# Gated linear attention and a gated MLP on one core: every chunk handled in pairs, attention's output summed already turned in 64x32 tiles

## The chip, the cores and the metric

The kernel runs on one core of a Trainium2 chip. The metric is the device time of one execution in microseconds (us); the kernel before takes 144.32 us, the median of three runs (144.17 to 144.49). TensorE multiplies matrices and writes to PSUM (eight banks of 128 partitions x 512 fp32 here), VectorE, ScalarE and GpSimd work on SBUF (GpSimd not on PSUM), and SyncE issues nearly all DMAs. In the profile these are PE (PEld for its weight loads), DVE, ACT, POOL and SP.

## The reference

```python
# attention: B=4, H=8, S=768, D=48, alpha in (0.8, 1)
for t in range(S):
    state = alpha[:, :, t, :, None] * state + einsum('bhd,bhe->bhde', k[:, :, t], v[:, :, t])
    y[:, :, t] = einsum('bhd,bhde->bhe', q[:, :, t], state)
x = y.transpose(0, 2, 1, 3).reshape(B, S, 384)
# gated MLP: d_ff = 1024, w_spatial is 768x768
h = maximum(x @ w_in, 0);  u, v = h[..., :512], h[..., 512:]
v_n = (v - mean(v)) / sqrt(var(v) + 1e-6)
v_s = einsum('ts,bsd->btd', w_spatial, v_n) + b_spatial[None, :, None]
out = (u * v_s) @ w_out
```

Inputs and output are fp32; matmuls work on bf16.

## The kernel before

**Attention in chunks.** A batch's 768 steps are six chunks of 128, 24 chunks in all. In a chunk the recurrence is turned into matmuls: the logarithm of alpha (`ln`) is summed over time by a matmul with a triangle of ones (`cum`), ScalarE takes exp(-sum) (`einv`) and exp(sum) (`eexp`, in place in PSUM), k is multiplied by the first (`kt`) and q by the second (`qt`). TensorE transposes both (`tr`, `trk`), DVE or ACT copy them to SBUF (`ev`, tile kqT). The scores (`sc`) are k against q for each head, masked on DVE (`m`, tile ptm). The output y of a chunk is scores times v plus q times the state at the chunk's start (`ya`, `y`). The state (`upd` on TensorE, `z` on DVE, decay `S` and block-diagonal bf16 copy `sb` on POOL) goes from chunk to chunk. The heads are taken two by two, `HP` = 4 pairs of heads, each head in 64 columns or rows of which 48 are used.

**Two forms.** The first eight chunks run in `pair(j)` (line 423, `PAIRS` in line 53): one load brings 256 steps, step 2p and 2p+1 side by side in partition p, so that 384 bytes lie together in memory. Chunk 0 of the pair is then partitions 0 to 63 and chunk 1 partitions 64 to 127, each with an even and an odd half (`par`). The sums over time take two matmuls for each half, with `le_pair` and `lt_pair` (line 461); `upd` (553), `sc` (583), `ya` (610) and `y` (623) take a chunk from half of the rows. The other 16 chunks run in `first(i)` (line 634), one chunk at a time: loads of 192 bytes a row, `cum` in line 666, totals in 669, transposes of k and q in 64-row halves (719), `upd` in 740, `sc` in 754, `y` in 776 (state part) and 782 (scores times v).

**To the MLP.** y stands in PSUM with time in the partitions. The MLP needs x with features in the partitions, so `finish_x` (line 356) has ACT copy y to x_sb, TensorE transpose it (374 in pairs, 398 elsewhere), and ACT or DVE copy it out into xT:

```python
363 def xs(eng):
364     st["x_sb"] = work.tile([128, KS, 128], BF16, name="x_sb")
365     copy(eng, st["x_sb"], st["y"]...)            # 128x384, fp32 to bf16
...
373     for ks in range(KS):
374         nc.tensor.transpose(xv[:, ks, :], st["x_sb"][:, ks, :], ident)
```

**The MLP.** All its matmuls have line 828: v (three of 512 columns for 128 steps), u (three of 384), the mixing s with w_spatial turned (six of 384; two steps `part 0` and `part 1` after the normalised v of tiles 0 to 3 and 4, 5), and the output o (four of 384). `second_v` has DVE take batch-norm statistics (893, 894), except for four tiles named in `ACT_STATS` (line 54), where ACT sums (879, 889) and DVE finishes (905 to 908). `se` adds the bias (976), `g` multiplies with u (989). Lines 197, 199 and 205 are the helpers for copies on ACT, on DVE or POOL, and relu on DVE. w_in, w_out and w_spatial are loaded in fp32 pieces and cast; w_spatial is turned by TensorE (`wt`, 840).

**The order.** Each step is an `Op` with its engine; the string `PLAN` lists all steps in the order in which they are issued, with the letter of the engine (P, D, A, G for GpSimd, S for SyncE). An engine does its own steps in this order and waits where an input isn't ready. A word such as `P53:512:512:192` puts fill matmuls ahead of a step: products of a constant fp32 tile (`junk`, line 187) of so many columns, whose result isn't used. PSUM banks are taken in turn.

Of the kernel before, what the change touches and what calls it, by code (L numbers as in the profile page):

```python
# [14 lines left out]

class Op:


    def __init__(self, key, eng, dur, emit, deps=(), prio=0.0, take=None, lat=0.13, cols=0):  # L20
        self.key = key
        self.eng = {eng: dur} if isinstance(eng, str) else dict(eng)
        self.emit, self.prio, self.lat, self.cols = emit, prio, lat, cols
        self.take = [take] if isinstance(take, Slot) else list(take or ())
        self.deps = [d for d in deps if d is not None]
        self.done = False
        self.big = False


class Ring:  # L30


    def __init__(self, bufs):
        self.bufs = bufs


class Slot:
    def __init__(self, ring):
        self.ring, self.users = ring, []


ENGINES = {
    "kt": {"POOL": 0.9},
    "vb": {"POOL": 0.48, "ACT": 0.42},
    "S": {"POOL": 0.5},
    "sb": {"POOL": 0.73, "DVE": 0.95},
    "vn": {"DVE": 0.42},
    "xe": {"ACT": 0.4},
    "ev": {"DVE": 0.34, "ACT": 0.48},
    "u": {"ACT": 0.39, "DVE": 0.49},  # L50
    "o": {"ACT": 0.4},
}
PAIRS = (0, 1, 2, 3)
ACT_STATS = ((2, 2), (1, 4))
LETTERS = {"P": "PE", "D": "DVE", "A": "ACT", "G": "POOL", "S": "SP", "Q": "DMA"}

PLAN = """
S34 Q35 S36 Q37 G32 G0 Q33 S38 Q39 S94 Q95 S40 Q41 A42 P53:512:512:192 A54 D1 D2 D56 P43 S96 Q97 S98 Q99 S100 Q101
S163 Q164 S4 Q5 S165 Q166 S167 Q168 P59:464 G58 G48 A44 A45 A55 D46 D57 D47 P249:304 P49 P61 A50 P51 D52 D60 A62 A102
A250 P71:304 P74 P113 P103 D72 D73 D76 D75 P63 P77:172 D65 A114 D116 P119:148 A104 A64 A115 A105 A78 G66 G67 G106 D107  # L60
D117 D68 P79 P81 P111 P121 P247 P109 G3 G69 A108 A82 A80 D120 D122 D112 D110 P83 A84 A171 D248 S169 Q170 S9 Q10 S307
Q308 P131 P134 D133 D136 D132 D135 G70 G118 P172:228 P182 P123:240 A183 A8 A173 A124 P137 P138 A139 A174 G7 G6 D125
P85 G126 D128 D185 G127 G129 G175 P88 P142 P140 A86 A184 D176 D186 A143 A89 P188 P190 P180 P144 P178 A141 A191 A145
A181 P146 G11 G12 S309 Q310 S311 Q312 D130 D87 D179 D90 D189 P157 A187 A177 A158 A147 A13 P197 P200 P192 D199 D201
D198 D194 D202 P151:196 P155 A315 A193 A91 P326 P316 A327 P203 P153 P204 G195 G196 G329 A317 A328 A318 P149 A205 A154
D159 D156 D152 D330 G319 P208 P334 A209 P206 D320 P332 P324 P210 P322 D92 D335 D325 D333 D148 A207 P212 A211 A150 P347
P215 P221 A213 A160 A222 A216 S14 Q15 P223 P227 S18 Q19 D93 D323 D161 D348 D349 D214 G16 G17 A224 A228 P225 P229 A226
A21 P232 A234 D231 D230 D233 G20 P235:300 P238 S313 Q314 G331 G321 P344 P336 S367 Q368 S369 Q370 S22 Q23 S371 Q372
A237 A236 D217 D162 D346 A240 D338 A239 A218 D219 D220 A375 A337 P251 P263 P259 P376 A377 A378 G339 P264 D345 D341
D265 P260 D261 P255 P252 A380 A25 A24 D381 D253 P256 D257 G340 G342 G379 S409 Q410 S373 Q374 S446 Q447 S411 Q412 S413  # L70
Q414 S415 Q416 S26 Q27 S480 Q481 S448 Q449 S482 Q483 S450 Q451 S484 Q485 P383 A385 A417 S452 Q453 S577 Q578 S486 Q487
S581 Q582 S579 Q580 S583 Q584 P244 P241 P350 A246 D384 D245 D242 D243 P390 P354 P418 D392 D391 A351 A355 G262 G343
A420 A382 G254 G266 P279 P352 P271 P356 P393 P272 A353 A357 A419 G421 A422 A394 P280 P361 P386 P275 P395 A362 A424
A396 A31 D273 D423 D281 D387 P425 D397 D427 D426 D363 G282 G388 P276 P358 D277 P398 G258 G389 G278 G30 A399 A454 A359
A28 A488 P405 P432 P267 P455 P401 A402 A457 A456 D29 P291 P489 P268 A490 A459 D406 D433 D400 D434 D360 P283 P428 D269
D460 A492 D429 D493 G458 G491 P435 A284 A292 A436 G274 G461 G270 G430 G431 S648 Q649 S617 Q618 S650 Q651 S611 Q612
S652 Q653 S613 Q614 S690 Q691 S615 Q616 S694 Q695 S654 Q655 S692 Q693 P287 P462 P437 P495 P403 D463 D464 D497 D496
A288 A439 A438 P440 A585 A441 A364 D404 P469 P498 P295 P465 P586 P303 D471 D470 D466 D500 D499 A296 A587 A588 A590
A304 P299 G494 G467 G468 G589 G592 D591 D442 P472 A473 P501 P407 P474 A502 A300 P503 P593 P596 A443 A505 A408 D475
D476 P477 A478 D504 D366 D594 D595 D445 D444 D597 D365 P506 P600 P515 D601 D516 A507 A479 A508 D509 D602 A656 A510  # L80
A619 P517 P525 P513 P519 P529 P657 P533 P620 D511 D512 P526 P530 A514 A659 A658 A621 A661 A622 A698 A624 D518 D520
D527 D531 D662 P545 P534 P699 A701 A700 A703 D625 G598 G599 G660 G626 G623 G528 D535 P546 D547 P630 P627 P664 P537
P603 D631 D665 D704 G548 A629 A628 G632 G663 A604 P538 P634 P605 S728 Q729 S762 Q763 S696 Q697 S730 Q731 S732 Q733
S764 Q765 S766 Q767 D539 A607 A666 A606 D635 D636 P541 P667 P542 G702 G532 P706 P671 D668 D543 D673 D672 G669 G536
G670 G544 G633 P608 P637 P521 A707 A736 A708 A638 P737 P713 P639 P522 P549 D714 D715 D641 D523 A770 A609 A705 A738
A739 G740 A640 A741 D742 P771 P550 P642 A772 P709 P744 A774 A643 A746 D710 D551 D775 D745 D644 G524 S858 Q859 S734
Q735 S929 Q930 S860 Q861 G773 G711 G552 G712 G743 G540 P716 P674 A717 A675 P561 P718 P676 P777 P553 A562 A678 A677
D719 D779 D720 D610 P679 P751 A778 A554 A866 A680 A645 A681 P780 D752 P747 D748 D753 D781 D782 P682 P867 P721 P754
A868 A869 A871 A722 A755 S768 Q769 S862 Q863 A723 A776 D683 D872 P573 P688 P684 G749 G750 G870 P756 P874 D646 D757
D875 D685 D758 A689 A574 D724 A876 P686 P783 P569 P881 A784 P785 A570 A787 A687 A725 D882 D786 D883 P759 P557 A760  # L90
P788 P565 P796 P798 P800 S1042 Q1043 S971 Q972 S892 Q893 S864 Q865 S898 Q899 S896 Q897 A979 A558 A789 A566 A937 A900
S894 Q895 S935 Q936 G873 S975 Q976 S931 Q932 S933 Q934 S973 Q974 S977 Q978 S1008 Q1009 S567 Q568 S1046 Q1047 S559 Q560
S1012 Q1013 S1010 Q1011 S1044 Q1045 S1014 Q1015 D727 D647 D761 D726 P794 P806 D790 A791 D799 D797 D795 D792 D793 D801
P901 P980 P802 P938 P877 P807 A902 A903 A907 A905 A981 A939 A940 A982 A944 A984 P810 P803 A942 G904 D878 G941 G879
D808 D906 D804 G805 G880 G809 G983 D985 D943 P822 P884 P811 D812 A885 P823 P908 P886 P945 D824 P814 P911 P815 D912
D909 D816 G813 G817 G913 G825 A910 A887 A888 A947 A946 P889 A1016 A890 P952 P915 P987 D953 D916 D954 P830 P1017 P831
P818 A988 A1019 A1050 A1018 D917 P948 P819 P1051 D949 A1021 A986 A989 D1022 D832 G950 P834 A1052 G951 G1020 P990 P842
P918 A835 A1054 D820 D991 D1055 A843 A919 P838 P1024 P994 P920 D1025 D921 D995 D996 A839 A1023 G914 G833 G1053 G992
S1048 Q1049 S575 Q576 S836 Q837 S844 Q845 S293 Q294 S289 Q290 S571 Q572 S305 Q306 S301 Q302 S555 Q556 A922 A1026 S297
Q298 S285 Q286 S840 Q841 P826 P955 P827 D828 A956 P1057 P957 P1031 D958 P1027 D1028 D1033 D1032 P997 P923 A1058 A1059  # L100
A959 P969 P1060 A1056 A998 P999 D1062 D1001 D1061 D970 G821 G829 G993 G1029 A1000 A924 P960 P846 P1034 A961 A847 G1030
P1063 A1035 A1064 P1002 P963 P1036 P1065 D925 D891 A1003 D962 D1066 P850 P967 A1067 A1037 D1004 A926 D928 P1068 A964
A1038 P1039 D927 D968 A851 A1005 A1069 A1040 D1006 D1041 D1007 D1070 P965 P854 P1076 P1080 P1078 P1074 D966 A1079 A855
A1071 A1081 D1075 D1072 D1073 D1077 P1094 P1082 P1106 P1086 P1083 P1098 P1095 P1090 P1102 P1087 P1107 P1091 P1103
P1110 P1099 P1111 D1096 D1084 G1085 D1088 D1097 D1108 D1092 D1093 G1089 P1113 D1104 G1109 G1105 D1112 D1100 D1101
P1117 P1121 S852 Q853 S563 Q564 S856 Q857 S848 Q849 A1114 S1115 Q1116 A1118 P1133 S1119 Q1120 A1122 P1125 A1134 S1123
Q1124 P1129 S1135 Q1136 A1126 P1137 S1127 Q1128 A1130 A1138 S1131 Q1132 S1139 Q1140
"""


def replay(ops, fill, plan):

    for word in plan.split():
        number, *junk = word[1:].split(":")
# [9 lines left out]
def kernel(  # L124
# [50 lines left out]
    def bank(shape):  # L175
# [5 lines left out]
        for x in shape[1:]:  # L181
            n *= x
# [111 lines left out]
    def op(key, *args, **kw):  # L294
# [3 lines left out]
        for s in users:  # L298
            s.users.append(o)
# [857 lines left out]
```

## Time and profile before

| | |
|---|---|
| median of 3 runs | 144.32 us |
| span of the profiled execution, first to last instruction | 142.7 us (the page gives no time beside the span) |
| granted TensorE clock | 1.000 |
| PE busy | 134.7 us, 1912 matmuls |
| PEld busy | 84.8 us |
| DVE busy | 118.3 us, 291 instructions |
| ACT busy | 109.3 us, 282 |
| POOL busy | 83.4 us, 146 |
| DMA | 28.64 MB in 89000 packets, 83728 of them under 512 bytes |

Busy times are unions of spans of one execution; a matmul's own time (326 ns with 384 columns) is longer than the spacing to the next, since matmuls overlap. Groups of instructions that the prediction counts, with mean ns of one: L461 16 recorded and L666 16 (sums over time, 384 columns), L669 52 and L545 32 (totals, 1 and 2 columns), L511 64 and L719 256 (transposes of k and q), L740 104 and L553 112 (state updates, 48 columns), L754 128 and L583 128 (scores, 128 columns), L782 128 and L610 128 (scores times v, 48 columns), L776 56 and L623 24 (state part of y, 96 columns), L374 24 and L398 96 (transposes of x). On DVE: L765 and L594 48 masks at 682, L976 31 at 551, L893 20 at 682 with L894 20 at 182, L199 27 kqT at 416 and 14 xT at 250, L205 18 relu at 545, L925 24 at 409, L700 and L490 24 q at 545 to 550, L339 and L337 20 at 350 to 353. On ACT: L197 24 x_sb at 489, 18 xT at 325 and 8 at 491, 21 kqT at 598; L203 14 relu of u at 494.

### The profile page before, as it was taken

What the parts mean: (1) busy time and instruction counts of PE and PEld (TensorE: products, weight loads), DVE (VectorE), ACT (ScalarE), POOL (GpSimd) and SP (SyncE); (2) the same over time, 40 slices, a digit from 0 to 9 for tenths busy, and PEclk for the clock granted to TensorE, in tenths of its full rate; (3) what the DMA queues carried; (4) which work ended last, traced back from release to release, by engine and by line L of the source; (5) the groups of instructions that cost most, each with busy time, mean ns of one, the idle gap of its engine ahead of it and who ended that gap; (6) DMA issues with size and microseconds to landing.
All of it is one profiled execution on the core that took longest, in us unless ns stands there. A gap on an engine that the chain in (4) does not pass through costs nothing.

```text
span 142.7 us, 4968 instructions
## 1 busy us (share of the span) xinstructions
PE 134.7 (94%) x1912; PEld 84.8 (59%) x1923; DVE 118.3 (83%) x291; ACT 109.3 (77%) x282; POOL 83.4 (58%) x146
## 2 busy tenths in 40 slices
PE   7999798899999999999999999999999989999990
PEld 3457575566577656675666665656666656566560
DVE  7279878989989699999998898989979779994940
ACT  3477759999888969889987999997978978940061
POOL 6703977366339776982389999410799993000720
PEclk9999999999999999999999999999999999999999
DMA  4999999999998999999999998999998794113045
GB/s 106 270 261 261 321 259 256 290 289 358 236 217 160 237 226 202 194 169 203 171 196 183 182 198 140 214 152 194 191 231 165 229 341 168 56 58 111 0 161 170
DMA packets 89000, 28.64 MB, mean 201 GB/s; under 512 B 83728, under 2 KB 87440, under 8 KB 88976
## 3 DMA queue, kind: packets, MB, share of 16 engines
q1 hardware_dynamic: 88944, 28.32, 91.3%
q8 instruction: 15, 0.25, 0.8%
q14 instruction: 9, 0.07, 0.2%
q0 software_dynamic: 32, 0.00, 0.0%
HBM read 23.60 MB, written 4.72 MB: 198 GB/s over the span
## 4 chain that ended last, share of the span: by engine, by line
PE 63%; SPq 9%; POOL 7%; DMA 6%; DVE 5%; ACT 4%; issue 3%; ACTq 0%; POOLq 0%; DVEq 0%
PE bank L828 46%; SPq L441 8%; DMA qc<-in_q_dram 6%; PE bank L719 2%; PE bank L754 2%; POOL kt L690 2%; POOL gT L989 2%; POOL sbd L199 2%; PE bank L782 2%; DVE ptm L765 1%; PE bank L740 1%; PE bank L666 1%; SPq L1081 1%; PE bank L776 1%; DVE qt L490 1%
## 5 line engine op out<-in xcount | busy, mean ns | idle before, releaser
L828 PE MATMUL bank<-w_spT,vn 128*128 128x384 bf16 x192 | 36.8, 326 | 0.0
L989 POOL TENSOR_TENSOR gT<-vsb,uT 128x384 bf16<-128x384 f32 x28 | 25.7, 925 | 14.9 <-DVE vsb L976 14.4
L765 DVE TENSOR_TENSOR ptm<-bank,mask 128x512 bf16<-128x512 f32 x32 | 20.7, 682 | 1.9 <-PE bank L398 1.2
L828 PEld LDWEIGHTS <-vn 128*128 128x128 bf16 x192 | 16.6, 97 | 9.5 <-issue 0.2
L690 POOL TENSOR_TENSOR kt<-kc,binv 128x384 bf16<-128x384 f32 x16 | 14.6, 915 | 9.9 <-ACT bc L685 5.1
L976 DVE TENSOR_TENSOR vsb<-bank,bsp_bc 128x384 f32<-128x384 f32 x31 | 16.5, 551 | 4.2 <-PE bank L828 2.5
L828 PE MATMUL bank<-xT,w_in 128*128 128x384 bf16 x96 | 18.7, 326 | 0.0
L828 PE MATMUL bank<-w_out_sb,gT 128*128 128x384 bf16 (+1 forms) x100 | 18.7, 319 | 0.0
L828 PE MATMUL bank<-w_in,xT 128*128 128x512 bf16 x61 | 17.1, 379 | 0.8 <-issue 0.2
L344 POOL TENSOR_TENSOR state<-state,bc 128x192 f32<-128x192 f32 x20 | 10.4, 522 | 8.9 <-ACT bc L559 3.4
L197 ACT COPY kqT<-bank 128x512 bf16<-128x512 bf16 x21 | 12.1, 598 | 3.7 <-PE bank L719 1.1
L199 POOL CAST sbd<-state 64x192 bf16<-64x192 f32 x38 | 13.3, 350 | 2.0
L893 DVE BATCH_NORM_STATS2 stats<-v_sb 128x6 f32<-128x512 bf16 x20 | 13.6, 682 | 0.3 <-ACT v_sb L203 0.3
L203 ACT ACTIVATE v_sb<-bank 128x512 bf16<-128x512 f32 x20 | 11.7, 604 | 1.2 <-PE bank L828 1.0
L828 PEld LDWEIGHTS <-w_in 128*128 128x128 bf16 x96 | 8.8, 97 | 5.9
L828 PEld LDWEIGHTS <-gT 128*128 128x128 bf16 x100 | 8.9, 97 | 5.6 <-DVE gT L989 0.4
L199 DVE COPY kqT<-bank 128x512 bf16<-128x512 bf16 x27 | 10.4, 416 | 1.9 <-PE bank L511 1.0
L197 ACT CAST x_sb<-bank 128x384 bf16<-128x384 f32 x24 | 11.4, 489 | 0.7 <-PE bank L610 0.2
L187 PE MATMUL bank<-junk 128*128 128x512 f32 (+9 forms) x24 | 10.5, 542 | 1.1 <-DVE junk L240 1.1
L197 ACT COPY xT<-bank 128x192 bf16<-128x192 bf16 (+1 forms) x26 | 9.3, 376 | 1.7 <-PE bank L398 1.1
L594 DVE TENSOR_TENSOR ptm<-bank,mask 128x512 bf16<-128x512 f32 x16 | 10.2, 682 | 0.5 <-PE bank L583 0.3
L197 ACT COPY o_sb<-bank 128x384 f32<-128x384 f32 x9 | 4.4, 484 | 8.0 <-PE bank L828 8.0
(126 smaller groups left out, 285.4 us busy)
## 6 DMA issues: line engine op xcount, KB each, us to landing
ac<-in_alpha_dram SPq DMA_DIRECT2D x16, 192.0 KB, 4.4
kc<-in_k_dram SPq DMA_DIRECT2D x16, 192.0 KB, 4.9
qc<-in_q_dram SPq DMA_DIRECT2D x16, 192.0 KB, 4.3
vc<-in_v_dram SPq DMA_DIRECT2D x16, 192.0 KB, 4.4
raw_w<-in_moe_w_spatial_dram SPq DMA_DIRECT2D x3, 768.0 KB, 6.7
out_dram<-raw_w SPq DMA_DIRECT2D x11, 192.0 KB, 2.7
out_dram<-o_sb SPq DMA_DIRECT2D x9, 192.0 KB, 1.9
ac<-in_alpha_dram SPq DMA_DIRECT2D x4, 384.0 KB, 6.2
```

The source lines that it names most:

```text
L187: nc.tensor.matmul(out=flat[:, 0:cols].rearrange("p (a b) -> p a b", a=4), lhsT=junk, rhs=junk[:, None, 0:n].to_broadcast([128, 4, n]), st ...
L197: nc.scalar.copy(out=out, in_=in_)
L199: ENG[eng].tensor_copy(out=out, in_=in_)
L203: nc.scalar.activation(out=out, in_=in_, func=AF.Relu)
L344: ENG[eng].tensor_tensor(out=st["state"], in0=st["state"], in1=st["bc"][:, :, None].to_broadcast([128, HP, D]), op=ALU.mult)
L441: nc.sync.dma_start(out=t.rearrange("p h a d -> p h (a d)"), in_=src[b, :, t0:t0 + 2 * C, :].rearrange("h (p a) d -> p h (a d)", a=2))
L690: ENG[eng].tensor_mul(out=k_blocks(kt3)[:, :, :, 0:D], in0=quad(st["kc"]), in1=st["binv"])
L765: nc.vector.tensor_tensor(out=st["ptm"][:, s], in0=st[f"pt{s}"], in1=mask4, op=ALU.mult)
L828: return lambda ps: nc.tensor.matmul(out=out(ps), lhsT=lhsT(), rhs=rhs(), start=start, stop=stop)
L893: nc.vector.bn_stats(out=stats, in_=d["v_sb"][:, tt, :])
L976: nc.vector.tensor_tensor(out=hold["vs"], in0=ps[:, 0:TH], in1=bsp_bc[:, th, :], op=ALU.add)
L989: ENG[eng].tensor_tensor(out=bt[b]["gT"][:, dsl, cols], in0=hold["vs"], in1=bt[b]["uT"][:, dsl, cols], op=ALU.mult)
```

## The change

`first` and the single-chunk loads go: all twelve pairs run in `pair`, rewritten. The second half's sum over time is no longer two matmuls: it is the first half's sum plus that step's own logarithm, on VectorE (`c1`). The transposes work in halves of 64 rows, `upd` in 64x64 tiles. The output sums are turned round: v is the stationary operand in pieces of 32 columns, the masked scores are the moving one with 128 columns, so that y comes out with features in partitions and time in columns; one copy (`xe`) brings it to xT. The state part of y goes the same way with the state in pieces of 32 columns. The statistics of v are all on VectorE. `sb` multiplies with the decay itself, beside `S`, which may run on VectorE. Time inside a chunk is kept in the order even, odd in xT and in all that follows; w_spatial's casts and copies, the bias and the output's stores take that order. Banks are named in the new order table (`@6,7`), which replaces the old one as a whole. The planner's leftover numbers (`pe=`) are not used when the kernel is built. The mask has one copy for four pairs of heads, read with a repeat. The diff, cut to its core:

```diff
-    def finish_x(i):
-        op(("xs", i), "ACT", 0.38, xs, got(("y", i), ("xt", i - WK)), ...)
-                    nc.tensor.transpose(xv[:, ks, :], st["x_sb"][:, ks, :], ident)
-    def first(i):
...
     def pair(j):
...
+        def cum(_):
+            cm = flat(sl_c[0])
+            for par in range(2):
+                nc.tensor.matmul(
+                    out=cm[:, 0:DM], lhsT=(le_pair, lt_pair)[par], rhs=la[:, par, :, :, 0:D],
+                    start=(par == 0), stop=(par == 1))
...
+        def tot(_):
+            cm = flat(sl_c[1])
+            for hp in range(HP):
+                for par in range(2):
+                    nc.tensor.matmul(
+                        out=cm[:, DM + 2 * hp:DM + 2 * hp + 2], lhsT=la[:, par, hp].rearrange("p s d -> p (s d)"),
+                        rhs=halves_of, start=(par == 0), stop=(par == 1))
...
+        op(("c1", j), "DVE",
+           lambda _: nc.vector.tensor_tensor(
+               out=quad(sums(1)), in0=quad(sums(0)), in1=la[:, 1, :, :, 0:D], op=ALU.add),
+           [("cum", j), ("tot", j)], use=sl_c)
...
+            def tr(_, n=n, src=src, cols=cols):
...
+                for par in range(2):
+                    for hp in range(HP):
+                        for r in range(2):
+                            rows = half(r)
+                            nc.tensor.transpose(
+                                to[r][:, HP * par + hp, :], src[rows, par, hp].rearrange("p s d -> p (s d)"),
+                                ident[rows, rows])
...
+        def upd(_):
+            tp = {i: view(sl_t[i], HP, D) for i in chunks}
             for hp in range(HP):
+                for par in range(2):
+                    for s in range(2):
+                        for i in chunks:
+                            rows = half(i % 2)
+                            nc.tensor.matmul(
+                                out=tp[i][half(s), hp, :], lhsT=kt[rows, par, hp, s, :],
+                                rhs=vbp[j % 3][rows, par, hp, s, 0:D], start=(par == 0), stop=(par == 1))
...
+            if c < NCH - 2:
+                op(("S", i), "POOL DVE", lambda e, ...: mul(e, state[i % 3], zs[i % 3], decay(slice(0, 128))), ...)
+            def sbf(e, i=i, decay=decay):
+                for s in range(2):
+                    mul(e, sbd[i % NB][half(s), :, s * D:s * D + D], zs[i % 3][half(s)], decay(half(s)))
...
+                            nc.tensor.matmul(
+                                out=pt[s][half(ci), hp, :].rearrange("p (a t) -> p a t", a=2), lhsT=kT[n2][rows, ci, par, hp, :],
+                                rhs=qT[n2][rows, ci, :, hp, :], start=True, stop=True)
...
+        def place(y, n):
+            return y[32 * (n % 4):32 * (n % 4) + 32, n // 4, :]
+
         def ya(_):
+            y = [view(sl, KS, 128) for sl in sl_y]
+            for turn in range(4):
                 for par in range(2):
-                        nc.tensor.matmul(
-                            out=T[2 * j + ci]["y"][:, h, :], lhsT=st[f"ptm{par}"][rows, h % 2, h // 2, :],
-                            rhs=st["vb"][rows, par, h, :], start=(h == 0 and par == 0), ...)
+                    for hp, x in SUMS[turn]:
+                        for ci in range(2):
+                            rows = half(ci)
+                            nc.tensor.matmul(
+                                out=place(y[ci], 3 * hp + (0, 1, 1, 2)[x]),
+                                lhsT=vbp[j % 3][rows, par, hp].rearrange("p s d -> p (s d)")[:, 32 * x:32 * x + 32],
+                                rhs=ptm[n2][rows, par, x // 2, hp, :], start=(turn == 0 and par == 0),
+                                stop=(turn == 3 and par == 1 and (2 * j + ci) % NCH == 0))
...
+            def yf(_, i=i, ci=ci):
+                y = banks[sl_y[ci].bank][:, 0:DM].rearrange("p (k t) -> p k t", k=KS)
+                for n in range(3 * HP):
                     nc.tensor.matmul(
-                        out=T[i]["y"][:, 2 * hp:2 * hp + 2, :].rearrange("p s d -> p (s d)"),
-                        lhsT=q_cols(slice(0, 128), hp, ci), rhs=sbd_bufs[(i - 1) % NB][:, hp, :], ...)
+                        out=place(y, n).rearrange("p (a t) -> p a t", a=2), lhsT=sbd[(i - 1) % NB][:, n // 3, 32 * (n % 3):32 * (n % 3) + 32],
+                        rhs=qT[n2][:, ci, :, n // 3, :], start=False, stop=(n >= 3 * HP - 4))
...
+            op(("xe", i), "ACT DVE",
+               lambda e, c=c, ci=ci: copy(
+                   e, xT[b % 3][:, c].rearrange("p k t -> p (k t)"), banks[sl_y[ci].bank][:, 0:DM]), ...)
...
-        on_act = (b, t0) in ACT_STATS
...
+               [("oe", n) + tail])     # stores: out[...].rearrange("(t a) m -> a t m", a=2)
```

The four turns of `SUMS` each name four pieces of 32 columns that end in four different groups of 32 partitions; with the two chunks of a pair (`ci`) that is eight tiles at a time, and each turn runs over the two halves `par`. In the new order table VectorE has all 24 statistics, 3 of 24 copies of x, 5 of 32 relu evictions of u, 19 of 48 evictions of k and q, 5 of 25 of the output, 5 of 16 decays and 3 of 20 copies of the state; ScalarE has the rest of the evictions (29 of k and q, 21 of x, 27 of u, 20 of the output). The fill words are `:512:512:184`, `:220`, `:408`, `:204`, `:248`, `:344` (ahead of the second `ya`, before the first v) and `:84` (ahead of the first u); before they were 512, 512, 192, 464, 304, 304, 172, 148, 228, 240, then 196 and 300 after the first v.

## The prediction

> **What bounds the kernel now.** The table of stretches comes first. Its columns are the stretch, its length, the busy time of each engine with the number of instructions, the granted TensorE clock, the DMA engines' share and the rate in GB/s.
>
> ```profile
> 0.00:22.80 22.80, 20.26 (x293) 12.48 (x295) 16.09 (x48) 14.15 (x29) 13.72 (x35) 1.00 1.09 243
> 22.80:41.00 18.20, 17.27 (x311) 11.35 (x312) 17.31 (x42) 16.77 (x41) 8.84 (x14) 1.00 1.07 295
> 41.00:77.00 36.00, 35.77 (x531) 22.82 (x532) 32.71 (x81) 30.84 (x85) 25.91 (x43) 1.00 1.05 192
> 77.00:95.00 18.00, 17.53 (x287) 11.34 (x289) 15.82 (x40) 17.04 (x48) 13.25 (x22) 1.00 1.09 179
> 95.00:121.50 26.50, 26.01 (x388) 16.65 (x390) 23.24 (x54) 22.69 (x59) 17.86 (x29) 1.00 0.92 211
> 121.50:139.10 17.60, 17.60 (x108) 10.13 (x109) 13.13 (x30) 7.20 (x22) 3.85 (x4) 1.00 0.21 77
> ```
>
> From 22.8 us on TensorE is busy almost throughout, at the full granted clock, but VectorE (17.31 of 18.20 us, later about 90%) and ScalarE stand close behind, and the DMA engines are full until 95 us. Next the chain of waits, in order of time, tells what holds the first stretch:
>
> ```profile
> 13.96 8.82 DMA qc<-in_q_dram
> 22.78 0.03 issue
> ...
> 22.88 1.02 DVE qt L490 x2
> ...
> 27.01 0.42 PE bank L583 x16
> ...
> 121.48 17.55 PE bank L828 x105
> ```
>
> Until 22.8 us the load of q for the third pair sets the pace, whatever TensorE does. After that the chain is mostly TensorE's, and 17.55 us at its end are big matmuls that the change leaves alone. The cost of an edit is therefore its TensorE time after 22.8 us. I take it from the timeline of TensorE (start, length, line, count):
>
> ```profile
> 17.31 0.64 PE L583 MATMUL bank<-kqT 48*64 48x128 bf16 x32 [0.39 <-DVE kqT L199]
> 30.30 0.57 PE L610 MATMUL bank<-vbp,ptm 64*128 64x48 bf16 x32
> 32.38 0.40 PE L511 MATMUL bank<-ident,qt 128*128 128x128 bf16 x4
> 33.23 0.33 PE L374 MATMUL bank<-ident,x_sb 128*128 128x128 bf16 x3
> 47.89 0.33 PE L776 MATMUL bank<-sbd,kqT 128*128 128x96 bf16 x4
> 48.06 0.36 PE L782 MATMUL bank<-vb,ptm 128*128 128x48 bf16 x8
> 50.10 0.65 PE L828 MATMUL bank<-w_spT,vn 128*128 128x384 bf16 x3
> 50.68 0.26 PE L398 MATMUL bank<-ident,x_sb 64*128 64x64 bf16 x6
> 50.89 0.28 PE L719 MATMUL bank<-ident,qt 64*128 64x64 bf16 x8
> 51.10 0.66 PE L828 MATMUL bank<-w_spT,vn 128*128 128x384 bf16 x3
> ```
>
> A run of n matmuls lasts n-1 spacings and one matmul's own time (0.18 to 0.33 us in the groups). So the spacing is 162 ns for 384 columns, 25 ns in L782, 42 in L776, 57 in L511, 55 in L374, 14 in L398, 13 in L719, 12.6 in L610, and (0.64-0.216)/31 = 13.7 ns in L583, where four 64x64 tiles work at once: 55 ns for four. Going from whole-array to tiled matmuls costs 50.68-(50.10+0.49) = 0.09 us, and going back 51.10-(50.89+0.10) = 0.11.
>
> **The change on TensorE.** All counts are of the groups in the profile (before) and of the diff's loops (after).
> - Transposes of x: 24 of 55 ns and 96 of 14 go: -2.7 us.
> - Decay sums: 32 matmuls of 162 ns become 24, since the second sum is no longer a matmul: -1.3. The totals go from 84 to 96 of 25 ns: +0.3.
> - Transposes of k and q in pairs 0 to 3: 64 of 57 ns become 128 of 13: -2.0. The others keep their form.
> - State updates: 104 at 25 ns (L740, same shape as L782) and 112 at about 13 to 26 (L553), 4.2 us, become 320 in 64x64 tiles, 96 groups of at most four. No row shows these tiles with 48 columns: a group lies between 25 ns (L782, same columns) and 55 (L583, same tiles). I take 40, the middle: 3.8 us, -0.4 (-1.8 to +1.1).
> - Scores: 128 of 26 ns (L754) become 256 of 13.7: +0.2.
> - Output sums (`ya`): 128 of 25 and 128 of 12.6, 4.8 us, become 96 groups of eight 64x32 tiles of 128 columns. The nearest row is L583: one group there loads 128 weight columns per row half and streams 2x128 columns from it; a new group loads the same 128 but streams 4x128. If streams run side by side it takes 55 ns (5.3 us), if two at a time, 110 (10.6). I take 55, as L583's two streams cost no more than one: +0.5 (to +5.8).
> - State part of y: 80 of 42 ns become 60 groups of four 128x32 tiles, 55 ns by the same argument (to 110): -0.1 (to +3.2).
>
> Sum: -5.5 us. Pairs 0 and 1 (1.15 us less each by transposes and sums) lie before 22.8 us, behind the q load, which stays twelfth in SP's order; so -3.2 counts. Against that, the table of before changes between whole array and tiles (or between tile shapes) 69 times by the trace, the new one 84 times by its order: 15x0.10 = +1.5. Net -1.7.
>
> **The page that speaks against it.** The Trainium skill (TensorE: Matmul & The Clock Gate, "Wait — 56ns, not 53.3ns?") says that starts of matmuls are never less than about 25 ns apart. L782 agrees with 25 for the whole array, L583 with 13.7 doesn't across tiles; eight tiles no row shows. By the page a group of eight would take 200 ns, and the sum would be that of the rival with the 25 ns floor.
>
> **The other engines.** VectorE, by count and mean: added are 12 second sums at about 0.55 (as L700's 0.545: 6.6 us; 0.35 to 0.68 by the nearest rows), four batch-norm statistics moved from ScalarE (4x0.86 = 3.5), five state decays and two state copies, three of x and five of the output (about 7.6); gone are 14 copies of xT (3.5), 13 relu evictions (7.1), 8 of kqT (3.3), one kt (0.6), some constants, small statistics and copies (about 3.4). I get 134.8 before and 134.6 after: equal. ScalarE loses 24 x_sb and 26 xT evictions (21.5 us) and the statistics (4.1), and gains 21 evictions of x at 0.489 (10.3) and 13 of u (6.4): with smaller groups about -10 of 132. GpSimd's state copies now multiply (0.35 each by L199, up to 0.52 by L344: 0 to +6 us), its own decays fall from 20 to 11 (-4.7): equal, and it idles 42%. Strided casts and the mask read with a repeat keep sizes and engines; I take 0 (-1 to +1 in all, TensorE covering them). The stores write rows in another order with as many bytes: 0 (to +0.8, 1.9 against 2.7 us to landing).
>
> In SP's queue 64 loads of 192 KB become 32 of 384 KB: half as many, larger packets, in the stretch with the DMA engines full at 180 to 190 GB/s. No wait after 30 us names a q, k, alpha or v load, so I count nothing, but it leaves more cover.
>
> **Waits.** After 22.8 us the matmuls at these spacings, the switches and the fill (L187, 1.3 us) leave about 2 us of idle. The fill after that point falls from 496 columns to 84: -0.6, half of what that would free. The trip from PSUM to ScalarE, back to TensorE and out again for each x is now one copy; waits on it (L398 1.6 us idle before it) mostly pass to v and u, which need the same x: -0.5. The new wait is the second sum: it stands in VectorE's queue behind whatever the table puts first, and ScalarE's exponentials of that half and the masks behind it wait; between pairs TensorE has other big matmuls, so 0 (up to 0.3 each, 9 pairs).
>
> Total: -1.7-0.6-0.5 = -2.8. The span becomes 142.7-2.8 = 139.9. The page gives no total for the profiled execution; the median of the runs is 1.6 us above its span, which I keep: **141.5 us** against 144.32. A difference of 0.2%, 0.3 us, is about what measurement can tell.
>
> **Rivals.**
> - Better by the table (0.18): update groups at 25 ns (-1.4), all the fill gone and the idle with it (-2): 138.1. For it: less wanted of ScalarE and DMA. Against: VectorE at 90%.
> - Slower, tiles share the stream (0.14): groups of eight and of four at 110 ns. Outside pairs 0 and 1 that is 80x55 ns + 51x55 ns = 7.2 us: 148.7. It decides from 76 ns (2.8 us over 131 groups). For it: no row has four streams from one row half. Against: L583.
> - The 25 ns floor (0.03): if each matmul starts L782's 25 ns after the last, whatever its tile, groups take 200 and 100 ns: 80x145+51x45 ns = 11.6+2.3 us, so 155.4. The 13.7 of L583 speaks against it.
> - Nothing gained, VectorE is the bound (0.20): its sum doesn't fall, in 22.8 to 41 us it is already full, and TensorE's 2.8 us come back as waits on masks and sums. Centre 144.3, 143.2 to 146 with the second sum's waits (9x0.3).
>
> **How the numbers follow.** The forecast has 0.45, own range 139.8 to 143.2. Faster: 0.45+0.18+0.07 of the VectorE case = 0.70; same 0.05; slower 0.08+0.14+0.03 = 0.25. The range 136.5 to 147.5 leaves out the floor, most of the slower tiles and the best end of the better table, some 0.15.
>
> **What would show it.** Right: no matmul reads x_sb; the `ya` run of 64 matmuls takes about 0.44 us plus one matmul, y's 12 about 0.17; VectorE's busy time stays within 3 us of 118.3, ScalarE's falls by 5 to 10 from 109.3; first v matmul near 21 to 23 us; the same 17 us of big matmuls at the end. Wrong: `ya` runs near 0.9 us or more; TensorE idle before tiled lines that wait for masks or the second sum; or a later start of pair 2.

## The result: slower by 62 us, some 44 of them after the last matmul

The changed kernel takes 206.12 us (median of 4 runs, 204.66 to 206.97), the kernel before beside it 144.41 (144.17 to 144.72): 1.4263 times as long, interval 1.4201 to 1.4326. The forecast was 141.5 with a range to 147.5.

The page of the kernel after, with the span, the busy times, and three of the rows of 40 slices (5.1 us each):

```profile
span 204.2 us, 6545 instructions
PE 138.6 (68%) x2769; PEld 83.2 (41%) x2769; DVE 124.7 (61%) x283; ACT 102.9 (50%) x243; POOL 84.1 (41%) x133
PE   7788788768989799979699788999997000000000
PEclk9965899999999999999879999999999955555555
DMA  6999999999999896492611111101111111111110
```

TensorE works for 157 us, not 139, and then 47 us pass with hardly any work on any engine, where the kernel before ends some 3 us after its last matmul. Rows of the table of stretches, with the same columns as before:

```profile
0.00:23.00 23.00, 18.54 (x325) 10.85 (x333) 14.18 (x44) 14.75 (x30) 10.10 (x26) 0.78 1.09 254
23.00:40.00 17.00, 13.06 (x326) 7.50 (x326) 12.89 (x30) 10.80 (x27) 6.84 (x10) 1.00 1.10 301
40.00:80.00 40.00, 35.49 (x830) 22.02 (x829) 36.35 (x79) 31.44 (x76) 25.31 (x38) 1.00 1.00 237
...
140.00:172.00 32.00, 17.20 (x108) 10.07 (x106) 10.73 (x22) 4.37 (x12) 7.41 (x8) 0.85 0.13 49
172.00:204.00 32.00, 0.00 (x0) 0.00 (x0) 0.00 (x0) 0.88 (x3) 0.00 (x0) 0.50 0.13 48
```

In the last 64 us the DMA engines stand at a share of 0.13 and 48 to 49 GB/s: 0.13 of 16 engines is two. Early on the granted clock is 0.78, where it was 1.00, and TensorE is no longer busy throughout from 23 us. The chain of waits ends with waits for the buffers of two stores, and SyncE's timeline (start, length) shows stores 3.3 to 3.9 us apart:

```profile
139.55 16.31 DMA out_dram<-raw_w
156.75 14.79 DMA out_dram<-o_sb
```

```profile
145.10 3.82 SPq L739 DMA_DIRECT2D out_dram<-w_row  x1
148.96 3.82 SPq L739 DMA_DIRECT2D out_dram<-raw_w  x1
...
183.53 9.76 SPq L739 DMA_DIRECT2D out_dram<-raw_w  x3
```

TensorE's new tiles answer to the spacings that the prediction worked with (chain of waits, 33 to 37 us):

```profile
33.41 0.67 PE bank L531 x64
34.08 0.46 PE bank L578 x24
34.53 0.23 PE bank L547 x8
34.76 1.91 issue
36.67 0.34 PE bank L547 x10
```

The 64 matmuls of `ya` (L531) take 0.67 us with the return from the tiles (0.12 to 0.17 in this trace): about 65 ns for a group of eight. The 1.91 us of "issue" in the middle of y's run (L547) is a wait for which the trace names no engine. Six such gaps make 5.8 us; before had none of 0.25 us or more.

### The profile page after: what moved, and what is told of

It is laid out like the page before. It is cut to its first block, busy times and chain, and to the rows that moved or that the text cites. A ratio compares the mean times of both kernels' runs of the same rounds, so it can differ in the third digit from the quotient of the medians.

```text
span 204.2 us, 6545 instructions
## 1 busy us (share of the span) xinstructions
PE 138.6 (68%) x2769; PEld 83.2 (41%) x2769; DVE 124.7 (61%) x283; ACT 102.9 (50%) x243; POOL 84.1 (41%) x133
## 4 chain that ended last, share of the span: by engine, by line
PE 30%; DMA 21%; DVE 12%; ACT 11%; issue 6%; SPq 5%; ACTq 0%; DVEq 0%
PE bank L562 19%; DMA out_dram<-raw_w 8%; DMA out_dram<-o_sb 7%; SPq L361 4%; DMA vc<-in_v_dram 4%; DVE ptm L512 3%; PE bank L531 2%; PE bank L441 2%; ACT kT L197 2%; PE bank L504 2%; DMA ac<-in_alpha_dram 2%; ACT xT L197 2%; PE bank L547 1%; ACT v_sb L203 1%; DVE stats L633 1%
## 5 line engine op out<-in xcount | busy, mean ns | idle before, releaser
L208 POOL TENSOR_TENSOR gT<-vs,uT 128x384 bf16<-128x384 f32 x28 | 25.3, 924 | 17.5 <-DVE vs L708 14.5
L208 POOL TENSOR_TENSOR sbd<-zs,bc 64x192 bf16<-64x192 f32 x34 | 17.5, 515 | 9.0 <-ACT qT L197 2.6
L708 DVE TENSOR_TENSOR vs<-bank,bsp_bc 128x384 f32<-128x384 f32 x31 | 16.4, 549 | 3.8 <-PE bank L562 2.7
L203 ACT ACTIVATE uT<-bank 128x384 bf16<-128x384 f32 x27 | 13.0, 492 | 7.4 <-PE bank L562 7.3
L403 ACT ACTIVATE binv<-bank 128x384 bf16<-128x384 f32 x24 | 11.6, 493 | 5.0 <-DVE bank L397 4.6
L208 DVE TENSOR_TENSOR qt<-qc,bank 128x384 bf16<-128x384 f32 x24 | 12.7, 546 | 2.0 <-ACT bank L406 1.4
L397 DVE TENSOR_TENSOR bank<-bank,la 128x384 f32<-128x384 f32 x12 | 6.7, 560 | 10.8 <-ACT binv L403 6.3
L197 ACT COPY kT<-bank 128x512 bf16<-128x512 bf16 x17 | 9.8, 595 | 7.0 <-PE bank L441 6.9
L650 DVE TENSOR_SCALAR vn<-v_sb,mvs,rstd 128x512 bf16<-128x512 bf16 x24 | 12.2, 528 | 1.6 <-ACT rstd L644 1.6
L504 PE MATMUL bank<-qT,kT 48*64 48x128 bf16 x384 | 10.4, 235 | 4.0 <-issue 2.1
L406 ACT ACTIVATE bank<-bank 128x384 f32<-128x384 f32 x24 | 11.8, 493 | 0.9 <-DVE bank L397 0.9
```

The costliest lines, as they stand in the source:

```text
L197: nc.scalar.copy(out=out, in_=in_)
L203: nc.scalar.activation(out=out, in_=in_, func=AF.Relu)
L208: ENG[eng].tensor_tensor(out=out, in0=in0, in1=in1, op=ALU.mult)
L403: lambda _, par=par, buf=buf: nc.scalar.activation(out=buf, in_=sums(par), func=AF.Exp, scale=-1.0),
L406: lambda _, par=par: nc.scalar.activation(out=sums(par), in_=sums(par), func=AF.Exp),
L504: nc.tensor.matmul(out=pt[s][half(ci), hp, :].rearrange("p (a t) -> p a t", a=2), lhsT=kT[n2][rows, ci, par, hp, :], rhs=qT[n2][rows, ci, ...
```

## The experiments

### The stores

Theory S: the store of rows in another order is what takes the time. Two edits of the changed kernel and one of the kernel before:

```diff
 # two stores: one of 64 rows for each parity
-  nc.sync.dma_start(out=out[...].rearrange("(t a) m -> a t m", a=2), in_=to[:, cols])
+  rows = out[...].rearrange("(t a) m -> a t m", a=2)
+  for x in range(2):
+      nc.sync.dma_start(out=rows[x], in_=to[half(x), cols])
 # rows in order: one plain store (rows stay permuted inside each tile of 128)
+  nc.sync.dma_start(out=out[...], in_=to[:, cols])
 # the kernel before with the changed kernel's store (rows permuted in the same way)
+  nc.sync.dma_start(out=out[...].rearrange("(t a) m -> a t m", a=2), in_=hold["o"])
```

> The changed kernel with every output store issued as two transfers of 64 rows (even and odd rows), so that the outermost step of the transfer is 64 and no longer 2; all else equal. Theory S (a transfer whose outermost step is 2 is dealt to 2 of the 16 DMA engines: DMA share 0.13 = 2/16, 48 to 50 GB/s, 25 stores x 3.8 us = 95 us from 95 us on): the stores fall to the 2 to 3 us of the kernel before, the span ends some 3 us after the last big matmul, 138 + 17.2 + 3.5 = 159 us, time 158 to 162. Rival R (stores are slow because their rows are scattered in HBM): stores stay near 3.8 us each, time 195 to 215.

> The changed kernel with each output store as one transfer of 128 rows in the order of the partitions (it leaves out putting the rows of a tile back in order). Theory S: as the run with two transfers, 158 to 162, at most 1 us from it either way (25 issues fewer on SyncE). Rival R (scatter): also 158 to 162, so the two tell apart with the run of two transfers: if that stays above 190 and this one falls to 160, it is the scatter; if both fall, it is the outermost step of 2.

> The kernel before with nothing changed but the pattern of its output stores, written as the changed kernel writes them (outermost step 2; rows inside a tile of 128 come out in another order). Theory S: 24 stores' worth of data at 48 to 50 GB/s, 4.72 MB / 49 GB/s = 96 us after the first store at 101 us: time 198 to 206. Rival R2 (the slow stores of the changed kernel come from its own schedule, for instance stores bunched behind late tiles): time 144 to 150.

Measured: 168.61 us with two stores (168.06 to 170.84, ratio 1.1652, interval 1.1594 to 1.1711), 164.31 with rows in order, and 206.36 for the kernel before with the new store, where it has 144.36 without. So the store alone costs the kernel before 62 us, and mending it gives the changed kernel 37.5 or 41.8. The rows are as scattered in the two-store form, so scatter isn't it: the outermost step of 2 is. The two mended runs lie above the 158 to 162 us that were expected, and 4.3 us apart where at most 1 was; that is not explained, but it is far from the 195 us and more of the rival. The DMA row of the kernel before with the new store, and the end of the two-store form, with the DMA engines back at 0.47:

```profile
DMA  6999999999999999999954611111111111111110
```

```profile
140.00:162.00 22.00, 16.72 (x106) 9.88 (x104) 10.50 (x21) 5.24 (x13) 7.39 (x8) 0.93 0.47 110
```

In the trace of after two packets of these stores are under way at nearly any time: 1536 bytes in 65 ns, 23.6 GB/s each, 47 GB/s together. The trace doesn't name a packet's engine. The Trainium skill (DMA: Bandwidth & Descriptors, "Why a DMA increments its semaphore by 16 and not by 1") says why: a transfer is cut over the largest number of engines, up to 16, that divides the slowest dimension of both sides. With a slowest dimension of 2 that is two engines, and the share of 0.13 agrees.

Some 20 us are left (24 with two stores). Eleven of them were there before the first store, which is issued at 95 us: the first matmul of the spatial mixing starts at 44.0 us in after and at 40.4 in before, the second batch's at 79.3 and 68.2. At the third batch's, 116.7 and 98.7, it is 18.

### The second sum's order

Theory C: the exponential of the first sum stands ahead of the second sum in the order table, and holds it up.

```diff
 # two stores, and in the seven pairs where it stood behind it, the second sum (c1) ahead of the first exponential (einv), in two of them with the totals (tot)
-A388 ... D387        # pair 5
+D387 A388
```

> The run with two transfers per store, and in the order table the second decay sum on VectorE moved ahead of the first half's exp(-sum) on ScalarE in the seven pairs where it stood behind (in two of them the totals move ahead too). In the trace of the changed kernel the sum began 30 ns after that exponential ended (20.48 to 20.51, 38.52 to 38.55, 63.17 to 63.20 us). Theory C (this order makes the sum wait, and the late second half delays transposes and scores): 1 to 4 us faster than the run with two transfers. Rival (the wait is covered by other work): within 0.8 us of it.

Measured: 171.49 us (ratio 1.1873, interval 1.1817 to 1.1928), 2.9 above the two-store form. Theory C falls: the second sum's waits for the exponential are gone (5.0 us of VectorE's), but its waits for the totals rise from 2.5 to 7.0 us, and the exponential's for the second sum from 4.6 to 7.4. The early half clock is longer too, 20.5 us against 13.6, so the 2.9 us aren't the order's alone.

### Natural rows, and three single causes

The changed kernel was given x in the order of time by its own eviction, so that stores, spatial weights and bias are plain again and the rows come out in their places. The next runs build on it.

```diff
-  xT[b % 3][:, c].rearrange("p k t -> p (k t)"), banks[...][:, 0:DM]
+  xT[b % 3][:, c].rearrange("p k (t a) -> p k a t", a=2),
+  banks[...][:, 0:DM].rearrange("p (k a t) -> p k a t", k=KS, a=2)
 # w_spT, its casts, b_sp and the stores without their rearrange
```

> The changed kernel with x written in the order of time by its own eviction (a strided copy out of the bank), so that the spatial weights, their casts, the bias and the stores are in plain order as in the kernel before, and the result is the reference's. Theory (the stores were 40 us, the rest is TensorE's waits): within 4 us of the run with rows in order, 160 to 166 us, a little lower if the copies of the turned spatial weights fall back from 547 to about 345 ns; first s at 42 to 44 us as there. Rival (the odd row order cost far more than the stores, by way of the slower copies): below 155 us.

Measured: 160.25 us (158.94 to 162.49), ratio 1.1081, interval 1.0971 to 1.1191. That is 4.1 us below the run with rows in order and 8.4 below the two-store form; where the row order costs that isn't shown. 16 us are left to explain. Lines of its table of stretches and of its chain of waits:

```profile
10.00:30.00 20.00, 17.00 (x431) 10.30 (x434) 16.95 (x37) 14.67 (x32) 9.67 (x16) 0.74 1.12 292
```

```profile
20.01 0.49 ACT binv L403
20.50 0.02 issue
20.52 0.57 DVE bank L397
...
26.43 0.59 ACT kT L197
27.03 0.04 issue
27.07 0.39 PE bank L441 x15
...
33.99 1.91 issue
35.90 0.43 PE bank L547 x16
```

Three things show. The clock is 0.74 from 10 to 30 us. The second sum (L397) starts only when ScalarE's exponential, which merely reads the same bank, has ended; and TensorE's transposes of q (L441) start only when ScalarE has copied k out of other columns of the same bank. And there are waits without a releaser. The Trainium skill (PSUM — Partial Sum Buffer, "PSUM bank collisions raise a hardware error") states a rule for the second: two engines on the same 32 partitions of one bank collide, reads too, so the compiler's back end puts a dependency between them. This trace agrees: 0.02 and 0.04 us from end to start. Each of the three was tried by itself:

```diff
 # half of ya: only the first positions of each pair's sums of v are added
-                for par in range(2):
+                for par in range(1):
 # more fill early
-P71@6,7:408   P122@0,4:204
+P71@6,7:512:512:512   P122@0,4:512:512
 # second sum on TensorE (in tot), none on VectorE
+  for par in range(2):
+      nc.tensor.matmul(out=cm[:, 0:DM], lhsT=le_pair, rhs=la[:, par, :, :, 0:D], ...)
```

> As the run with natural rows, but each pair's sums of v leave out the second half of the positions (32 of the 64 matmuls of a pair; what they add to x is left out). Their own work is 12 x 32 x 8.1 ns = 3.1 us. Theory F (TensorE also waits for its own instructions, because a group of 64 tiny matmuls with 64 weight loads uses up one 16 KB packet of 256 instructions in 1.3 us, no longer than the packet takes to come): 768 x 2 = 1536 instructions less, 15 instead of 21 packets, the gaps without a releaser fall from about 6 us to below 2.5, and the time falls by 6 to 9 us. Rival (those gaps are hidden or have another cause): the gaps stay at 4 us or more and the time falls by 3.5 us at most.

> As the run with natural rows, with 2.2 us more of the fill matmuls in the waits of the first pair (8 to 13 us), so that TensorE's busy time there is no lower than in the kernel before. Theory G (the clock is halved from 12 to 28 us because TensorE is idle for half of 8 to 12 us): the granted clock is 0.95 or more over 10 to 30 us, and the time falls by 2 to 5 us. Rival (the small tiles are what lowers the clock, or the transfers set the pace until 40 us): the clock stays near 0.6 there or the time changes by less than 1 us.

> As the run with natural rows, with the second decay sum made by TensorE again (two more 128x384 matmuls per pair, 12 x 0.325 = 3.9 us) and none of it on VectorE (12 x 0.56 = 6.7 us less, and no wait of it for binv). Theory P (TensorE's own stream with its waits sets the time): 2 to 5 us slower. Rival V (VectorE, 36 of 40 us busy in the middle, and the second sum's waits of 8 to 10 us are what sets the pace): 2 to 7 us faster.

Measured, one run each beside 160.25 (whose own runs spread over 3.6 us):
- Half of `ya`: 156.15, so 4.1 less, of which 3.1 is the matmuls' own time. The gaps without a releaser fell from 2.5 to 1.8 us only. Theory F is not borne out by this run, but the test is weak: the edit leaves out 768 instructions and 3 of 21 packets, half of what was expected, and the gaps were 2.5 us and not about 6 to begin with.
- More fill: 161.92. The clock over 10 to 30 us rose from 0.74 to 0.85 (theory G expected 0.95), the time didn't fall, and the gaps without a releaser rose from 2.5 to 5.4 us. This run doesn't bear out the clock as a single cause, but the clock wasn't whole in it either.
- Second sum on TensorE: 158.16, 2.1 less although TensorE has 3.9 us more to do. This points to V, but it is one run, 0.8 us below the lowest of the other kernel's four, and its clock over 10 to 30 us is 0.91, not 0.74: V and the clock aren't told apart here.

### Another order for the same operations

If the loss is waits of an order that didn't reckon with them, a better order should give it back. Only the order table is changed, here against the run with natural rows (first words):

```diff
-S52 D0 G4 D3 A56 S103 D2 A107 P57@0:512:512:184 P58@1 ...
+922 words for the same 922 operations, in another order; some 90 on another engine
```

> The run with natural rows with the same operations in another order table: TensorE's order, the engine of some 90 copies and products, and the banks are chosen again by a search that uses the durations of that run's trace and lets two engines have one bank of sums only one after the other, as the trace shows them to (TensorE's second turned tile starts 0.03 us after ScalarE's kT copy out of the same bank ends; VectorE's second decay sum starts 0.02 us after ScalarE's binv out of the same bank ends). Theory O (the 16 us that are left are waits of an order that did not reckon with the shared banks and with these durations; the operations themselves fit): 146 to 151 us, TensorE's idle time halved. Rival W (the waits come from instruction packets, the clock and transfers, whatever the order): 156 us or more.

> The run with the second decay sum on TensorE, its order searched again in the same way. Theory O: 148 to 153 us, and some 2 us above the other new order, as TensorE sets the time again and does 3.9 us more. Rival V (VectorE's second sum is what holds the kernel up in any order): 2 us or more below the other new order.

Measured: 161.76 us (ratio 1.1177, interval 1.1105 to 1.1248) and 160.72. Theory O is not borne out by these orders: neither is faster, and rival V's 2 us don't show between them either. The waits and the clock of the first one (its profiled execution was 4 us above the median) show where the gain went:

```profile
PE bank L243 <- ACT binv L392: 3.3, 1, 3.3
PE bank L536 <- issue: 2.9, 2, 2.1
PE bank L453 <- issue: 2.9, 1, 2.9
```

```profile
PEclk9965555559999997799579999999999999999998
```

L243 is the fill, L536 y, L453 the updates. After 12 us TensorE waits little for any engine. But in this trace a wait of 3.3 us from 8 us on (fill behind an exponential for its bank) was followed by half the clock until about 36 us, and the gaps without a releaser grew to 7.8 us. A third table reckons with these two, and the packets have a run of their own, in which x takes in the sums of v three times:

```diff
 # three times ya
-            for turn in range(4):
+            for turn in range(12):
...
-                    for hp, x in SUMS[turn]:
+                    for hp, x in SUMS[turn % 4]:
```

> The run with natural rows, its order table searched once more, now also reckoning with what the first new order's trace showed: a packet of 256 of TensorE's instructions can be used about 1.4 us after it has landed, some 3 to 5 us after it was wanted, so that at most 256 tiny instructions may follow each other in that time; and the clock is halved after a few us with little full-array work, so that waits of the first 45 us are filled with fill matmuls (47 words, 21 us of them, in place of 9 words and 4.5 us). Theory FC (instruction packets and the clock are what the first new order lost by): 146 to 151 us, granted clock 0.98 or more, less than 1.5 us of gaps without a releaser. Rival (something else holds the changed kernel at 156 to 160 us): 155 us or more.

> The run with natural rows, with every pair's 64 matmuls of v's sums made three times in a row (x takes in the sum three times). Their own work is 12 x 128 x 8.1 ns = 12.4 us, and 12 x 256 = 3072 more instructions with their weight loads, 12 more packets. Rival (the packets are no bound): 170 to 174 us. Theory F (no more than 256 instructions in the 3 to 5 us from wanting a packet to using it, where the tiles alone would use 256 in 1 us): 188 to 205 us, and a gap of 1 us or more without a releaser in nearly every pair, each ending 1.3 to 1.7 us after a packet has landed.

Measured: 168.06 us for the order with fill (ratio 1.1533, interval 1.1439 to 1.1628), not the 146 to 151 of theory FC. Whether FC is right this run doesn't decide: the early half clock is gone (0.968 in the mean), but TensorE had been given so much fill that its own stream is 91% of the chain, and 7.5 us of gaps stayed, where less than 1.5 was expected. By 23 us it had done 3.3 us of its real work; the run with natural rows had done 5.2, the kernel before 9.1.

Three times `ya` took 214.26 us, 54.0 more than once, for 12.4 us of matmuls. Theory F holds here, beyond the upper end of what it expected. Some 33 of the 54 us are gaps without a releaser; the half clock also lasts 48 us here, against 10. TensorE's timeline and its waits:

```profile
83.92 1.63 PE L531 MATMUL bank<-ptm,vb 64*32 64x128 bf16 x171
89.59 0.35 PE L531 MATMUL bank<-ptm,vb 64*32 64x128 bf16 x21 [4.05 <-issue]
```

```profile
PE bank L531 <- issue: 28.1, 12, 4.1
PE bank L547 <- issue: 4.4, 2, 2.2
```

The DMA queues of two neighbouring pieces of that wait, 84.0 to 86.5 us and 86.5 to 87.8:

```profile
q1 hardware_dynamic: 1709, 0.65, 127.6%
```

```profile
q1 hardware_dynamic: 543, 0.20, 69.2%
q8 instruction: 1, 0.02, 5.5%
```

171 matmuls run in 1.63 us, then TensorE stands for 4.05. The queue of instructions (q8) has nothing under way at first and then one packet of 16 KB, by the trace from 86.84 to 87.97 us; 1.62 us after it has landed the run goes on. From the first of the 192 to the last it is 5.81 us, 30 ns each with the wait. The same holds for 70 of the 72 gaps of 0.25 us or more without a releaser in the thirteen profiled kernels with the new tiles: each ends 1.12 to 1.68 us after such a packet landed (median 1.45). In the other two, of 0.26 and 0.33 us, the matmul had a semaphore to wait for. There are 15 packets in before, 21 in after and 33 here, 257 to 264 TensorE instructions for each. A group of eight tiles is 16 instructions in 65 ns, so a packet's worth lasts about 1 us, less than the 2.2 us and more from a packet's start to its first use. What starts a packet the runs don't show.

### Three waits less at once

```diff
 # second sum on TensorE and more early fill as above; in the table, in four pairs
-P288@6,3 A289 P291      # tr k, copy of k, tr q (pair 3)
+P288@6,3 P291 A289
```

> The run with natural rows with three suspected waits taken away together, in the changed kernel's own order table otherwise: the second decay sum on TensorE (3.9 us more of its work, no wait of VectorE and ScalarE for each other on the sums' banks), q's turned tiles issued directly behind k's before either bank is copied out (in the four pairs where they waited 2.8 us in all for ScalarE's kT copy), and the 2.2 us more of early fill. Theory S (the rest of the loss is a sum of such small waits, which each give back a part): 154 to 158 us, 2 to 6 below the run with natural rows. Rival (what one wait gives back the next takes, as in the two new orders): 159 us or more.

Measured: 158.71 us (157.37 to 162.66), ratio 1.0954, interval 1.0852 to 1.1056, which overlaps that of natural rows. The transposes no longer wait for the kT copy; at `ya` (L523 here) and the scores (L496) this stands in its place:

```profile
PE bank L523 <- issue: 4.2, 3, 2.2
PE bank L496 <- issue: 1.2, 2, 0.9
```

The gaps without a releaser are 6.3 us where they were 2.5. Counting all of TensorE's waits of 0.15 us or more ahead of its own work, those that a named engine ended fell from 12.5 to 3.0 us, and those without a releaser rose from 2.7 to 6.5. The second sum's matmuls add 3.9 us and the fill 0.9. So the named waits were worth some 9 us; the packets took 4 of them, and what was put on TensorE to be rid of them took 5.

## Why the prediction was wrong, step by step

**"The stores write rows in another order with as many bytes: 0 (to +0.8 ...)"** is the step that failed by far the most. It counted bytes and the time to landing, not over how many engines a transfer is cut. The runs put it at +62 us alone and 38 to 42 in this kernel; the rule of the Trainium skill told above would have shown it in the diff.

**The TensorE terms were right in kind.** Work by count and spacing fell by 6.5 us (5.5 forecast). The groups of eight take 65 ns (55), y's groups of four 48 (55), the updates' 32 (40). Changes between tilings went up by 19 and cost 2.5 us (15 and 1.5). For runs of 64, the 25 ns floor is wrong: 8.1 ns from matmul to matmul. "No matmul reads x_sb" holds, ScalarE's busy time fell by 6.4 us (5 to 10 forecast). VectorE's rose by 6.4, where it was to stay within 3: 24 normalizations at a mean of 528 ns, not 409, are 2.9 us of it. That no wait after 30 us names a load of q, k, alpha or v was misread: in before GpSimd waits 4.3 us for one of v until 58.9 us, though TensorE stands for 0.5 us in all after 40.

**"Waits on it ... -0.5" and "0 (up to 0.3 each, 9 pairs)"** is the second failed step. TensorE's stream, from start to start, in us (work is count by spacing; a wait behind fill counts as fill):

| | before | natural rows | three waits less | new order, with fill |
|---|---|---|---|---|
| work | 111.7 | 105.2 | 109.1 | 104.7 |
| changes of tiling | 7.6 | 10.1 | 10.1 | 12.2 |
| fill | 9.7 | 10.8 | 11.7 | 26.9 |
| waits and stretched intervals | 9.0 | 26.0 | 20.0 | 18.1 |
| of these, gaps before a packet | 0 | 2.5 | 6.3 | 7.5 |
| span | 142.7 | 156.9 | 155.8 | 167.8 |

The work is that of the recorded matmuls; 11 to 15 matmuls of 512 columns have no record (2.4 to 3.2 us), and their time stands under waits. The span has 5 to 6 us more than the sum, ahead of the first matmul and behind the start of the last.

With natural rows the waits grew by 17 us, and the saving of work is lost in them. The forecast took the first stretch as paced by loads and let the change come free there; the first matmul of v was to start at 21 to 23 us and starts at 24.9 in after (21.3 in before). In fact the kernel before had 21.6 us of its work done at 40 us, the changed one 15.0: both then have 90 left, for which before takes 103 us and the other 117. After 40 us the clock is whole in both; in the waits of 0.15 us or more TensorE stands for 8.6 us there with natural rows, 5.3 of them ended by ScalarE and 2.7 by VectorE, and for 0.5 in before. The largest waits of TensorE's own work for a named engine, over the whole run, in before and (three lines) with natural rows:

```profile
PE bank L583 <- DVE kqT L199: 0.8, 2, 0.4
```

```profile
PE bank L441 <- ACT kT L197: 2.8, 4, 1.1
PE bank L504 <- DVE kT L199: 1.3, 1, 1.3
PE bank L531 <- DVE ptm L512: 1.2, 1, 1.2
```

**The rivals.** "VectorE is the bound" put the centre at 144.3; undoing its second sum, for 3.9 us more of TensorE's work, moved the time by 2 us at most. VectorE ended 4.9 us of TensorE's 15.2 us of waits with natural rows and ScalarE 7.1, so it isn't VectorE alone. "Tiles share the stream" is refuted by 65 ns. None of the rivals had a transfer on two engines or TensorE short of instructions. The 25 ns floor, at 155.4 nearest to the natural rows' 160, is refuted as a rule from matmul to matmul; what the packets do to the longest run (30 ns each with the wait) is another mechanism.

By the trace of natural rows, 13 of the 17 us are waits of 0.15 us or more (15.2, where before has 2.1), the gaps before packets among them; some 3 are matmuls stretched by the half clock, estimated from the spacings. **What stays open** is what each of them costs in time. The packets (1.8 to 7.8 us by kernel, the tripled `ya` aside), the halved clock early and the banks that engines take in turn are seen in the traces, but taken away singly or together, with what that put on TensorE, they gave back 2 us at most. Three other orders were no better, so it isn't shown that any order of these operations reaches 144 us; none of the kernels here beats the one before.

## What to carry to other kernels

Before a transfer is rearranged, look at its outermost step: it sets over how many DMA engines the transfer is cut, and an outer 2 left a DMA share of 0.13, two of 16. Count the instructions of small tiles as well as their time: a long run of them is paced by how fast instruction packets come, not by the matmuls. A saving on the busiest engine is worth only what its next wait leaves, so cost a change to an order table by the waits that it makes, the engines that share a bank among them.

## What the runs showed of the hardware

- A store of 128 rows of 1536 bytes with an outer step of 2 runs at a DMA share of 0.13, two engines' worth, at 47 to 50 GB/s; as two stores of 64 rows it doesn't (share 0.47 at the end).
- Eight 64x32 tiles work at once: 65 ns for eight matmuls of 128 columns, and 8 ns per matmul in 64x64 tiles with 48 columns.
- TensorE's program comes in 16 KB packets of some 260 instructions, about 1.2 us each while loads run, first used 1.1 to 1.7 us after landing where TensorE waited for one. Three `ya` runs in a row spend 36 us in 16 waits for them.
- In one trace a wait of 3.3 us from 8 us on was followed by half the clock for 27 us. Matmuls were busy for 23.0 of them, 12.5 on small tiles.
